# Putting the opening loads of a fused attention and MLP block on one queue, in the order of need

## The chip, the cores and the metric

The kernel runs on one core of a Trainium2 chip. The metric is the device time in microseconds (us). A number of us is the median over the fast runs of a kernel, unless the text says "profiled"; a profiled execution has a span of its own, some 1.7 us shorter than the device time of that same run. The engines are TensorE (matrix multiplications, "PE" in the profile; its weight loads are "PEld"), VectorE ("DVE"), ScalarE ("ACT"), GpSimd ("POOL") and SyncE ("SP"), which issues most transfers.

## The reference, cut to what matters

```python
x = A_x                                   # 1 x 2048 x 640, bfloat16
xn = _layernorm(x, axis=-1)               # (x - mean) / sqrt(var + eps)
return x + _A_ref(xn, A_wqkv, A_w_phi, A_wo) + _B_ref(xn, B_w1, B_w3, B_w2)
# _A_ref: qkv = xn @ wqkv; features of q and k are softmax(k @ w_phi) and softmax(-k @ w_phi) in 32 heads
#         of 20 columns; linear attention over them with v; result @ wo
# _B_ref: (silu(xn @ w1) * (xn @ w3)) @ w2
```

The 2048 tokens are 16 tiles of 128. The kernel starts from nothing, so it has an opening: the first tiles of x have to be loaded and normalised, and the weights of the features have to be folded (wk times the block diagonal of w_phi), before the main stream of projections can run.

## The kernel before: the parts that matter

The program is a list of operations (in the code cuts of this document, `...` marks what is left out, and most comments were added here). Each has a cost in us per engine that can run it, written by hand. A list scheduler plays through these costs and so decides which engine does what, and in which order. What it decided is then emitted with semaphores. A transfer is costed too, by a simple model of one shared bus. So a change to a transfer's place or cost can move instructions on every engine.

```python
POOLED = (0, 1)          # tiles whose normalisation runs on GpSimd
SEED = 0                 # the scheduler's random seed for the first 25 us
...
def bus(o, elem):        # the scheduler's cost of a transfer
    ...
    return n * 2 / elem / 16 * max(18.0, 10 + 0.0352 * elem) + 100.0
...
def ln_stats(t0, n, level):
    # DVE: bn_stats x2, bn_aggr (mean and variance); then 1/sqrt(var + eps) on GpSimd:
    ...
    add([w_op("POOL", "tensor_scalar_add", (r, v, EPS), 0.21, 0.25)], [r], [v], None, level)
    add([w_op("POOL", "tensor_tensor", (r, r, mhalf[:, 0:n], ALU.pow), 0.55 + 0.1 * (n - 1),
              0.6 + 0.1 * (n - 1))], [r], [r, mhalf[:, 0:n]], None, level)
...
def ln_apply(t, level):  # x_tok <- (x_tok - mean) * rstd, in place
    o, m, s, z = x_tok[:, t, :], mv[:, t, 0:1], mv[:, t, 4:5], mv[:, t, 6:7]
    ways = [w_op("DVE", "tensor_scalar", (o, o, m, s, ALU.subtract, ALU.mult), 0.35, 0.44)]
    if t in POOLED:
        ways = [w_op("POOL", "tensor_scalar", (o, o, m, s, ALU.subtract, ALU.mult), 1.25, 1.3)]
    ...
def block_diag(level):   # BDc: w_phi masked to a block diagonal, five products on GpSimd, read by every fold
    for c in range(DC):
        ...
        add([w_tt("POOL", o, a, b, ALU.mult, n * DH)], [o], [phi_s[:, c, :], GF[:, c, :]], None, level)
```

For the first four tiles the V projection does not wait for the normalisation. It runs on x minus its mean (`xc`, transposed to `xcT`), and the result is scaled by rstd afterwards. The K projection needs the normalised `x_tok`, transposed to `xnT`. TensorE's opening is then: transposes of xc0 and xc1, V0 and V1, transposes, V2 and V3, transposes, five folds into `Wkp`, and from there K projections and the MLP with the rest behind them.

The opening loads of before; "SP" is the default queue, and the last number in a call sets the priority:

```python
load_x(0, 1, lv)
load_x(1, 2, lv - 1)
...
load_wv(0, 2, lv - 2, "SP")
load_x(2, 3, lv - 3)
load_wv(2, 5, 2e9, "ACT")               # 480 KB at once, issued by ACT at the start
load_x(3, 4, lv - 4)
load(phi_s[:], phi_t, 2e9 - 1e3, "ACT")
for e in range(DC):
    load_wT(1, e, lv - 9 - e)           # wk, turned during the transfer: five transposes
load_w13(0, 256, lv - 16)
n = len(P.all)
load_x(4, 8, 1.9e6, "ACT")              # tiles 4-7, 640 KB
late(n, 9.0)                            # not before 9 us, by the scheduler's clock
```

The softmax here doesn't subtract the row's maximum and nothing guards it: scores larger than these inputs give would overflow.

## Time and profile before

| | before |
|---|---|
| device time, median of 3 runs (range) | 276.52 us (276.46 to 276.59) |
| span of the profiled execution | 274.9 us |
| TensorE busy | 266.7 us, 97% of the span |
| first fold starts | 15.78 us |
| first K projection starts | 17.60 us |
| from there to the end of the span | 257.3 us |

The page of before: the span, TensorE's busy time (busy us, share of the span, instructions), and the shares of the chain of waits over the whole span. That chain is followed back from the last instruction to what released it, again and again.

```profile
span 274.9 us, 5053 instructions
PE 266.7 (97%) x2078; PEld 158.9 (58%) x2097; DVE 183.1 (67%) x319; ACT 102.6 (37%) x187; POOL 65.7 (24%) x103
...
PE 91%; POOL 3%; ACT 2%; DVE 1%; issue 1%; DMA 1%
```

TensorE is the bound. In the opening, before 17.60 us, it stands idle for 3.9 us, and single holes are over 1 us long. In the 257.3 us behind that it is idle for 4.3 us in all, in short holes; the longest that its table of waits shows is 0.3 us.

The chain of waits of before, in the window from 0 to 18 us. The columns are start in us, length in us, and what it was.

```profile
by line: POOL x_tok L580 28.1%; PE PS L572 26.8%; DMA x_tok<-in_A_x_dram 12.6%; POOL mv L580 11.2%; PE PS L787 5.6%; DVE bst L580 4.9%; issue 2.6%; DVE xc L580 2.0%; PE PS L757 1.6%; DVE mv L580 0.7%
...
0.81 2.27 DMA x_tok<-in_A_x_dram
...
3.11 0.89 DVE bst L580 x2
...
5.74 2.53 POOL x_tok L580
...
8.57 0.78 POOL mv L580 x2
9.36 2.53 POOL x_tok L580
...
11.93 0.45 PE PS L787 x5
```

The opening hangs on x0's load, then on DVE's statistics, and then on GpSimd until 11.88 us. GpSimd normalises x0 (2.53 us), computes rstd of tile 1, and normalises x1 (2.53 us). No load but x0's is on this chain.

TensorE's timeline of before. The columns are start us, us, engine, line, operation, output <- inputs, shapes and count; in brackets is the idle time before it and what ended that.

```profile
6.85 2.88 PE L572 MATMUL PS<-wv,xcT 128*128 128x320 bf16 x20 [0.58 <-ACT xcT L580]
...
11.93 0.45 PE L787 MATMUL PS<-ident,x_tok 128*128 128x128 bf16 x5 [1.64 <-POOL x_tok L580]
...
15.78 1.87 PE L572 MATMUL PS<-BDc,wqkT 128*128 128x140 bf16 x30
17.60 0.85 PE L572 MATMUL PS<-Wkp,xnT 128*128 128x320 bf16 x5
```

V0 starts at 6.85, when ACT has copied xcT (6.84); wv's last piece had landed at 6.72. The longest wait that TensorE has once it works is 1.64 us, for GpSimd's x_tok. The folds start at 15.78.

GpSimd's timeline of before, first and last of its opening work, and then two lines of DVE's:

```profile
4.57 0.24 POOL L580 TENSOR_SCALAR mv<-mv 128x1 f32<-128x1 f32 x1 [2.28 <-DVE mv L580]
...
13.66 1.59 POOL L580 TENSOR_TENSOR BDc<-phi_s,GF 128x140 bf16<-128x140 bf16 x4
```

```profile
7.36 0.50 DVE L580 BATCH_NORM_STATS2 bst<-x_tok 128x6 f32<-128x320 bf16 x1 [1.16 <-DMA x_tok<-in_A_x_dram]
...
12.82 0.44 DVE L580 TENSOR_SCALAR x_tok<-x_tok,mv 128x640 bf16<-128x640 bf16 x1
```

Between these two GpSimd lines no other line has a bracket: GpSimd works without a hole from 4.57 to 15.25. DVE waits 1.16 us for the load of x2 until 7.36, and by that delays tile 1's statistics, but GpSimd is busy with x0 until 8.27 anyway. The last line shows what the same normalisation costs on DVE: 0.44 us for tile 2, against 2.53 on GpSimd.

The transfers issued by before in the first 10 us, from the profile's table of issues (output <- input, queue, kind, count, KB each, median us from issue to landing):

```profile
x_tok<-in_A_x_dram SPq DMA_DIRECT2D x4, 160.0 KB, 4.0
...
wv<-in_A_wqkv_dram ACTq DMA_DIRECT2D x1, 480.0 KB, 4.2
wv<-in_A_wqkv_dram SPq DMA_DIRECT2D x1, 320.0 KB, 5.0
```

### The profile page before, as it was taken

To read this page: it belongs to the slowest core of one execution; us is meant where nothing else is said; L and a number is where in the kernel's file an instruction comes from. 1 tells how busy PE (TensorE), PEld (TensorE's weight loads), DVE (VectorE), ACT (ScalarE), POOL (GpSimd) and SP (SyncE) were. 2 spreads that over 40 slices of the span, in tenths; PEclk is the share of its full clock that TensorE was granted. 3 is DMA by queue.
4 is the path that set the end of the run, shared out by engine and by line. 5 is a ranking of instruction groups with operands and counts; after the bars stand their busy time and mean duration, and the time that the engine had idled before them with its cause. 6 is when DMAs were issued, how large, how long until landed. Compare 5 with 4: busy or idle time off the path is not lost.

```text
span 274.9 us, 5053 instructions
## 1 busy us (share of the span) xinstructions
PE 266.7 (97%) x2078; PEld 158.9 (58%) x2097; DVE 183.1 (67%) x319; ACT 102.6 (37%) x187; POOL 65.7 (24%) x103
## 2 busy tenths in 40 slices
PE   6799999999999999999999999999999999999996
PEld 3575477656654447544444445677777774444774
DVE  4698989999957433678978978577661215666112
ACT  6379377564553451256673382010000002222000
POOL 5923556999997000000000000000000000000000
PEclk9999999999999999999999999999999999999999
DMA  7999997910000000803211111243332222000001
GB/s 216 237 317 347 195 132 129 187 67 0 2 0 2 0 0 2 284 6 27 47 26 24 38 36 24 75 99 95 97 96 75 72 72 74 0 0 0 26 24 48
DMA packets 41255, 21.98 MB, mean 80 GB/s; under 512 B 27024, under 2 KB 41232, under 8 KB 41232
## 3 DMA queue, kind: packets, MB, share of 16 engines
q1 hardware_dynamic: 39648, 20.49, 31.2%
q10 hardware_dynamic: 1584, 1.17, 1.5%
q8 instruction: 16, 0.26, 0.4%
q14 instruction: 7, 0.06, 0.1%
HBM read 12.81 MB, written 2.62 MB: 56 GB/s over the span
## 4 chain that ended last, share of the span: by engine, by line
PE 91%; POOL 3%; ACT 2%; DVE 1%; issue 1%; DMA 1%
PE PS L572 91%; POOL x_tok L580 2%; ACT EqT L580 2%; DMA x_tok<-in_A_x_dram 1%; POOL mv L580 1%; PE PS L787 0%; DVE bst L580 0%; DVE hT L580 0%; DVE den_s L580 0%; DVE xres L580 0%; ACT e_s L580 0%; DVE xc L580 0%; PE PS L757 0%; DVE t L580 0%; DVE pr_s L580 0%
## 5 line engine op out<-in xcount | busy, mean ns | idle before, releaser
L572 PE MATMUL PS<-xnT,w_s 128*128 128x512 bf16 x465 | 105.6, 379 | 1.4 <-issue 0.5
L572 PEld LDWEIGHTS PS<-xnT,w_s 128*128 128x128 bf16 x480 | 46.4, 98 | 54.5 <-DVE hT L580 0.8
L572 PE MATMUL PS<-w_s,hT 128*128 128x320 bf16 x384 | 55.0, 299 | 0.0
L580 ACT ACTIVATE th<-PS 128x512 f32<-128x512 f32 x48 | 28.7, 599 | 66.0 <-PE PS L572 66.0
L580 DVE SCALAR_TENSOR_TENSOR t<-th,PS 128x512 bf16<-128x512 f32 x48 | 32.6, 679 | 24.0 <-ACT th L580 23.9
L572 PEld LDWEIGHTS PS<-w_s,hT 128*128 128x128 bf16 x384 | 37.1, 98 | 14.9
L580 DVE TENSOR_TENSOR xres<-PS,xres 128x640 bf16<-128x640 f32 (+1 forms) x17 | 13.4, 786 | 41.2 <-PE PS L572 41.2
L580 POOL TENSOR_TENSOR ekt<-ekt,rS 128x640 bf16<-128x640 bf16 x32 | 39.6, 1275 | 1.5 <-DVE rS L580 1.5
L580 DVE SCALAR_TENSOR_TENSOR hT<-t,PS 128x512 bf16<-128x512 bf16 x48 | 32.5, 677 | 1.3 <-PE PS L572 0.3
L580 ACT ACTIVATE EqT<-PS 128x512 bf16<-128x512 f32 x40 | 21.9, 594 | 12.6 <-PE PS L572 12.6
L580 DVE TENSOR_REDUCE S<-ekt 128x64 f32<-128x1280 bf16 x16 | 22.9, 1458 | 3.4 <-ACT ekt L580 3.4
L572 PE MATMUL PS<-wo_s,oT 128*128 128x320 bf16 x160 | 24.5, 299 | 0.0
L580 DVE TENSOR_TENSOR prod<-PS,g_s 128x1280 bf16<-128x1280 f32 x16 | 23.8, 1490 | 0.5
L580 ACT ACTIVATE ekt<-PS 128x640 bf16<-128x640 f32 x32 | 20.8, 701 | 8.6 <-PE PS L572 8.4
L572 PE MATMUL PS<-Wkp,xnT 128*128 128x320 bf16 x160 | 23.9, 299 | 0.0
L572 PE MATMUL PS<-xnT,Wqp 128*128 128x512 bf16 x96 | 23.1, 380 | 0.3 <-issue 0.2
L580 ACT ACTIVATE e_s<-PS 128x64 f32<-128x64 f32 x32 | 9.1, 284 | 37.6 <-PE PS L572 37.1
L572 PEld LDWEIGHTS PS<-wo_s,oT 128*128 128x128 bf16 x160 | 15.7, 98 | 6.1
L572 PEld LDWEIGHTS PS<-Wkp,xnT 128*128 128x128 bf16 x160 | 15.5, 98 | 6.0
L572 PE MATMUL PS<-wv,xnT 128*128 128x320 bf16 x120 | 18.3, 299 | 0.0
L580 DVE BATCH_NORM_STATS2 bst<-x_tok 128x6 f32<-128x320 bf16 x32 | 14.3, 469 | 3.0 <-DMA x_tok<-in_A_x_dram 3.0
L572 PEld LDWEIGHTS PS<-xnT,Wqp 128*128 128x128 bf16 x100 | 9.3, 98 | 10.8
(68 smaller groups left out, 172.1 us busy)
## 6 DMA issues: line engine op xcount, KB each, us to landing
w_s<-in_B_w_dram SPq DMA_DIRECT2D x4, 640.0 KB, 9.2
xres<-in_A_x_dram SPq DMA_DIRECT2D x16, 160.0 KB, 2.2
out_dram<-xres SPq DMA_DIRECT2D x15, 160.0 KB, 1.8
w_s<-in_B_w_dram SPq DMA_DIRECT2D x1, 1920.0 KB, 9.2
w_s<-in_B_w_dram SPq DMA_DIRECT2D x4, 320.0 KB, 5.5
x_tok<-in_A_x_dram SPq DMA_DIRECT2D x2, 640.0 KB, 8.4
wo_s<-in_A_wo_dram SPq DMA_DIRECT2D x1, 800.0 KB, 4.9
x_tok<-in_A_x_dram SPq DMA_DIRECT2D x4, 160.0 KB, 4.0
```

Of the source, the lines that this page charges most:

```text
L572: return nc.tensor.matmul(o(u.k), l, r, start=start, stop=stop, skip_group_check=shared)
L580: return getattr(e, name)(*[at(a, u) for a in args], **{k: at(v, u) for k, v in kw.items()})
```

## The change

The intent is that data which is needed first should land first. The big 480 KB piece of wv no longer runs beside x0 and x1, on ACT's queue. It is cut in two and put behind them on SP's queue. phi and tiles 4 to 7 are issued later. The scheduler's bus model and its seed are changed as well.

```diff
-SEED = 0
+SEED = 1
...
-        return n * 2 / elem / 16 * max(18.0, 10 + 0.0352 * elem) + 100.0
+        return n * 2 / elem / 16 * max(18.0, 12 + 0.0375 * elem) + 100.0
...
     load_wv(0, 2, lv - 2, "SP")
     load_x(2, 3, lv - 3)
-    load_wv(2, 5, 2e9, "ACT")
-    load_x(3, 4, lv - 4)
-    load(phi_s[:], phi_t, 2e9 - 1e3, "ACT")
+    load_wv(2, 3, lv - 4, "SP")
+    load_wv(3, 5, lv - 5, "SP")
+    load_x(3, 4, lv - 6)
+    n = len(P.all)
+    load(phi_s[:], phi_t, 2e9, "ACT")
+    late(n, 4.0)
     for e in range(DC):
         load_wT(1, e, lv - 9 - e)
     load_w13(0, 256, lv - 16)
     n = len(P.all)
     load_x(4, 8, 1.9e6, "ACT")
-    late(n, 9.0)
+    late(n, 10.3)
```

Because the schedule is built anew, instructions move too. A comparison of the two built programs shows it. On GpSimd, tile 2's rstd comes before x1's normalisation, and tile 3's comes before the first BDc block. On TensorE, tile 1's transpose stands directly before V2, and behind the folds its matmuls come in the same order as before. DVE has one copy less in the opening and two instructions less in all, which ACT takes over, and a different order. No arithmetic of the block is added or removed; TensorE gets five more of the warm-up matmuls on zeros that it runs before V0 (22 instead of 17).

## The prediction

> **What bounds the kernel now.** TensorE: the page gives it 266.7 of 274.9 us (97%), the chain of waits is 91% matmuls of line 572. From 17.60 us (first K projection) the timeline shows TensorE almost without a hole, at clock 1.00. So only the opening can give anything: whatever moves the folds (15.78 us) and K (17.60 us) moves the end nearly one for one.
>
> **What bounds the opening.** The chain of waits: x0's load 0.81 to 3.08, DVE statistics to 4.5, then GpSimd: 0.25 + 0.76 (rstd of tile 0), 2.53 (normalise x0), about 1.0 (rstd 1), 2.53 (normalise x1) to 11.88; then TensorE: transposes, V2 and V3 (2.72), transposes, folds. The timeline shows GpSimd without a hole from 4.57 to 15.25, when the last BDc block (needed by the first fold) is done. TensorE's longest wait, 1.6 us, is for GpSimd's x_tok. The loads bind less: V0 starts at 6.85, when wv's SP piece lands (1.73 + 5.0), and DVE waits 1.2 us for x2 until 7.36, which holds tile 1's statistics until 7.95; but GpSimd is busy until 8.27.
>
> **What the change does.** wv's 480 KB on ACT's queue moves behind x0, x1, wv[0:2], x2 on SP's. Per the Trainium skill (DMA: Bandwidth & Descriptors, "Issuing engines are not separate DMA queues") both run on the same 16 engines and interleave. The trace agrees: x1 needed about 3 us, x0 2.27. 1305 KB landed between 3.08 and 7.8 us, some 280 KB per us. Estimates from that and 0.45 us per issue: x1 3.6 (was 4.3), wv[0:2] 4.8 (6.7), x2 5.4 (7.3), wv[3:5] 7.1, x3 7.7. V0 starts near 6.3, tile 1's statistics end near 6.5. x0 gains almost nothing: it took 2.27, the same 160 KB as xres 2.2.
>
> The price: weight transposes issue 0.6 us later (last lands near 14.5, needed near 16); tiles 4-7 land near 16 (needed 18.2). Both have slack.
>
> Rebuilding the schedule reorders instructions. On GpSimd, tile 2's rstd (0.24 + 0.75, partly overlapped) now stands before x1's normalisation, tile 3's before the first BDc. Same work, same start: x0 done 8.27, rstd 1 and 2 until 10.05, x1 done near 12.6 (was 11.88), BDc done near 15.5. TensorE now has tile 1's transpose directly before V2 and V3: 12.65 + 0.28 + 2.72 + 0.28 = 15.95 for the folds, against 15.78. What the loads win (0.5 us at V0, 1.5 us at tile 1's statistics) turns into a longer wait for GpSimd. Behind the folds TensorE's order is the same.
>
> **Prediction.** -0.1 (x0) + 0.15 (folds) and jitter: 276.5 us; 275.7 to 277.3 in 8 of 10 cases. Faster by over 2%: 1%; within: 98%; slower: 1%.
>
> **Signs.** Right: x1, wv[0:2], x2 land 0.7 to 2 us sooner; V0 starts before 6.6; GpSimd gapless from about 4.5 to 15.5; x1's normalisation starts near 10.1; TensorE waits over 1 us for x_tok before V2; K starts at 17.4 to 18.1. Wrong: GpSimd has a hole or its normalisation gets shorter than 2.53; K before 17.2.
>
> **What would make it wrong.** Faster: x0 lands sooner, moving the whole GpSimd chain, or rstd 2 overlaps more. Slower: from 9.7 to 12.6 TensorE does only short transposes; the skill (TensorE: Matmul & The Clock Gate, Part 1) has the clock halved after an idle window of about 3.4 us. The 1.64 us hole here did not slow V2; a longer one could, costing up to 2.7 us. Or late weight transposes delay the folds.

## The result and the profile after

| | before | after |
|---|---|---|
| device time, median of 4 runs | 276.55 us | 276.93 us |
| range | 276.46 to 276.84 | 276.74 to 276.99 |
| span of the profiled execution | 274.9 us | 275.3 us |
| first fold starts | 15.78 us | 15.95 us |
| first K projection starts | 17.60 us | 17.66 us |
| from there to the end of the span | 257.3 us | 257.6 us |

The ratio is 1.0011, with a 95% interval from 0.9993 to 1.0028: the same within 2%, and not resolved from 1. A ratio here is the mean time of one kernel's fast runs over that of the other's of the same rounds, so it is not quite the ratio of the medians that are quoted.

The page of after:

```profile
span 275.3 us, 5067 instructions
PE 267.4 (97%) x2083; PEld 159.1 (58%) x2102; DVE 180.7 (66%) x317; ACT 103.7 (38%) x189; POOL 65.7 (24%) x103
...
PE 78%; DVE 10%; POOL 5%; issue 3%; ACT 2%; DMA 1%; POOLq 0%; DVEq 0%
```

TensorE does the same work but for the five warm-up matmuls. But DVE's share of the chain of waits went from 1% to 10%, so something in the main stream now touches DVE. That comes back below.

The transfers that after issued in its first 10 us:

```profile
x_tok<-in_A_x_dram SPq DMA_DIRECT2D x4, 160.0 KB, 3.0
wv<-in_A_wqkv_dram SPq DMA_DIRECT2D x2, 320.0 KB, 4.3
wv<-in_A_wqkv_dram SPq DMA_DIRECT2D x1, 160.0 KB, 3.6
```

The change did to the loads what it meant to: a tile of x now takes 3.0 us (median) instead of 4.0. The Trainium skill says in "DMA: Bandwidth & Descriptors", section "Issuing engines are not separate DMA queues", that transfers started by different engines run on the same 16 engines and interleave. This trace agrees: with the 480 KB of wv no longer issued beside it, x1 needed about 2.3 us instead of about 3.

The chain of waits of after, 0 to 18 us:

```profile
0.81 2.24 DMA x_tok<-in_A_x_dram
...
5.54 2.66 POOL x_tok L580
...
8.50 0.79 POOL mv L580 x2
...
9.36 0.64 POOL mv L580
...
10.01 2.53 POOL x_tok L580
...
12.68 0.44 PE PS L787 x5
```

It is the same chain. The step at 9.36 is new: rstd of tile 2 stands ahead of x1's normalisation, which starts at 10.01 instead of 9.36. Such times on GpSimd are rough, but the wait that they cause on TensorE is not. TensorE's timeline of after:

```profile
6.14 0.98 PE L572 MATMUL PS<-wv,xcT 128*128 128x320 bf16 x6
8.22 2.06 PE L572 MATMUL PS<-wv,xcT 128*128 128x320 bf16 x14 [1.10 <-DMA wv<-in_A_wqkv_dram]
...
11.11 0.45 PE L787 MATMUL PS<-ident,x_tok 128*128 128x128 bf16 x5 [0.27 <-DVE x_tok L580]
...
12.68 0.44 PE L787 MATMUL PS<-ident,x_tok 128*128 128x128 bf16 x5 [0.81 <-POOL x_tok L580]
...
15.95 1.87 PE L572 MATMUL PS<-BDc,wqkT 128*128 128x140 bf16 x30
17.66 0.72 PE L572 MATMUL PS<-Wkp,xnT 128*128 128x320 bf16 x4
```

V0 starts 0.71 us sooner, then stalls 1.10 us for the last piece of wv, which landed at about 8.1. Part of the earlier start is luck. The warm-up matmuls come at half pace at first (one of 128 columns every 0.11 us, later every 0.056), and how long that lasts differs from profile to profile: the last slow one started at 3.8 us in before, at 4.4 in after, but at 6.0 in phi_later and 6.8 in order_only, which come below. In after_x4_early, with the same loads before V0, V0 started at 6.93. Whatever is left of the gain is waited off at 12.68, for GpSimd. The folds start 0.17 us later than before, and K 0.06 us.

The other quarter of a microsecond lies far from the opening. TensorE's and DVE's timelines of before, around 63 us, with DVE's last two hT (a block of the MLP's hidden layer):

```profile
63.72 1.52 PE L572 MATMUL PS<-Wkp,xnT 128*128 128x320 bf16 x10
```

```profile
58.49 0.62 DVE L580 SCALAR_TENSOR_TENSOR hT<-t,PS 128x512 bf16<-128x512 bf16 x1
...
63.28 0.62 DVE L580 SCALAR_TENSOR_TENSOR hT<-t,PS 128x512 bf16<-128x512 bf16 x1
```

The same of after, and the only wait of TensorE's weight loads that its table of waits shows between 33 and 68 us (total us, times, longest):

```profile
63.78 1.78 PE L572 MATMUL PS<-Wkp,xnT 128*128 128x320 bf16 x10
```

```profile
63.48 0.62 DVE L580 SCALAR_TENSOR_TENSOR hT<-t,PS 128x512 bf16<-128x512 bf16 x1
```

```profile
PEld PS L572 <- DVE hT L580: 0.3, 1, 0.3
```

In both programs the first two matmuls of this K projection each wait for DVE, because they write to banks that DVE has to have read first: the second waits for an hT. But it is not the same hT. The two programs, built anew, show it. Both write this projection to the same two banks, but the MLP blocks ahead of it got their banks in another turn. So in before the bank was last read by the hT of 58.49, which had ended at 59.11, and in after by the next hT, the one of 63.48. In before the second matmul's weights are loaded at 63.72, while the hT of 63.28 still runs, and ten matmuls take 1.52 us. In after TensorE arrives only 0.06 us later, but its second weight load stands idle until that hT ends, and starts at 64.15. The ten matmuls take 1.78 us, a hole of about 0.26 us. It comes from the turn of the banks, not from a slower DVE. This and the 0.06 us of K make up the 0.3 to 0.4 us between the two spans. The hole also explains the 10% of DVE: from it the chain of waits is followed back along DVE and what feeds it, to about 28.7 us. So a tenth of the chain stands for a loss of 0.26 us.

### The profile page after: what moved, and what is told of

The parts are those of the page before. It is cut to its first block, busy times and chain, and to the rows that moved or that the text cites. A ratio compares the mean times of both kernels' runs of the same rounds, so it can differ in the third digit from the quotient of the medians.

```text
span 275.3 us, 5067 instructions
## 1 busy us (share of the span) xinstructions
PE 267.4 (97%) x2083; PEld 159.1 (58%) x2102; DVE 180.7 (66%) x317; ACT 103.7 (38%) x189; POOL 65.7 (24%) x103
## 4 chain that ended last, share of the span: by engine, by line
PE 78%; DVE 10%; POOL 5%; issue 3%; ACT 2%; DMA 1%; POOLq 0%; DVEq 0%
PE PS L572 78%; DVE S L580 4%; POOL mv L580 2%; POOL x_tok L580 2%; ACT EqT L580 2%; DVE hT L580 1%; DVE rS L580 1%; DVE bst L580 1%; DMA x_tok<-in_A_x_dram 1%; DVE t L580 1%; DVE x_tok L580 0%; ACT th L580 0%; ACT x_tok L580 0%; DVE mv L580 0%; POOL epsc L580 0%
## 5 line engine op out<-in xcount | busy, mean ns | idle before, releaser
L580 ACT ACTIVATE th<-PS 128x512 f32<-128x512 f32 x48 | 28.7, 597 | 65.7 <-PE PS L572 65.6
L572 PEld LDWEIGHTS PS<-Wkp,xnT 128*128 128x128 bf16 x160 | 15.4, 98 | 6.2 <-DVE hT L580 0.3
```

Source lines behind the costliest of these rows:

```text
L572: return nc.tensor.matmul(o(u.k), l, r, start=start, stop=stop, skip_group_check=shared)
L580: return getattr(e, name)(*[at(a, u) for a in args], **{k: at(v, u) for k, v in kw.items()})
```

## The experiments

In all experiments that move loads or instructions, the schedule of one kernel was kept as it was computed and only the named items were moved in it, so that the other engines keep their order. Every kernel gave a correct result. Before ran beside each of them, at 276.55 to 276.62 us. "K" is the start of the first K projection in the profiled execution, and "rest" is that span less K.

| kernel | median us (runs) | range | ratio to before, 95% | K | rest |
|---|---|---|---|---|---|
| before | 276.55 (4) | 276.46 to 276.84 | | 17.60 | 257.3 |
| after | 276.93 (4) | 276.74 to 276.99 | 1.0011, 0.9993 to 1.0028 | 17.66 | 257.6 |
| loads_only | 278.06 (6) | 277.43 to 280.89 | 1.0068, 1.0038 to 1.0099 | 19.56 | 257.3 |
| order_only | 276.99 (5) | 276.78 to 277.09 | 1.0012, 0.9999 to 1.0025 | 17.77 | 257.5 |
| phi_later | 276.91 (5) | 276.86 to 276.97 | 1.0011, 0.9999 to 1.0023 | 17.68 | 257.5 |
| norm_dve_after | 275.66 (5) | 275.50 to 275.83 | 0.9966, 0.9954 to 0.9978 | 16.56 | 257.3 |
| loads_only_again | 277.72 (4) | 276.45 to 277.91 | 1.0029, 1.0011 to 1.0046 | 18.64 | 257.4 |
| loads_only_filled | 277.49 (6) | 276.74 to 278.89 | 1.0032, 1.0013 to 1.0051 | 18.46 | 257.3 |
| norm_dve_before | 275.46 (6) | 275.22 to 276.31 | 0.9961, 0.9949 to 0.9974 | 16.37 | 257.3 |
| true_cost_after | 276.86 (5) | 276.70 to 277.15 | 1.0009, 0.9997 to 1.0021 | 18.05 | 257.3 |
| loads_only_x4_late | 277.23 (6) | 276.72 to 278.29 | 1.0030, 1.0013 to 1.0047 | 17.62 | 258.7 |
| after_x4_early | 276.85 (5) | 276.73 to 276.94 | 1.0011, 0.9998 to 1.0024 | 17.44 | 257.7 |
| norm_dve_wv_first | 276.15 (5) | 275.80 to 276.30 | 0.9981, 0.9967 to 0.9994 | 17.00 | 257.4 |

Each K and rest comes from one profiled execution. K differs by 0.2 us between profiles of one order (17.44 in after_x4_early, 17.68 in phi_later), so differences of 0.1 us are not resolved. The column "rest" already says much: it is 257.3 or 257.4 in every kernel but two kinds. It is 257.5 to 257.7 wherever after's order of instructions is kept, and 258.7 in one kernel that starves DVE.

The theory was: GpSimd's normalisation of x0 and x1 bounds the opening, so loads that land sooner are waited off there. The rivals were: the loads do bind, and the change gives with one hand what it takes with the other (x sooner, the end of wv and the weight transposes later); or it is the new order of instructions that costs what the loads win.

### loads_only: the new loads, with before's order on every compute engine

```diff
--- before
+    # the schedule stands; only the opening loads are moved
+    wv_2, wv_34 = piece(2, 3), piece(3, 5)        # SP, behind x2's load, instead of the 480 KB on ACT
+    ...                                           # each matmul waits for the piece that it reads
+    move(phi_load, acts[1])
+    move(x4_load, acts[6])
```

> The changed kernel's loads under the earlier kernel's instruction order on every compute engine. Theory A (GpSimd's gapless chain sets the opening, loads do not bind; the added 0.3 us came from the reordering): x1, wv[0:2] and x2 land as early as in the changed kernel, but GpSimd is gapless from about 4.5 to 15.2 us, K starts at 17.5 to 17.7, no hole before the K tile at 63.7 us, time 276.3 to 276.7 (ratio to the kernel before 0.999 to 1.001). Theory B (the loads bind, and what they gained was lost because wv[3:5] and x3 landed about a us later than estimated): the late wv[3:5] stalls V0 here too, so K starts 0.3 us or more later than 17.60.

It was slower than both kernels: 278.06 us, ratio 1.0068. Theory B had expected a late K, but through a stall of V0 for wv, and of that this profile shows at most 0.2 us. The profiled run has two lines that explain its own time. TensorE's timeline, V2 and V3:

```profile
12.90 4.55 PE L572 MATMUL PS<-wv,xcT 128*128 128x320 bf16 x20
```

And busy time by stretches of 1 us (the stretch and its length; then TensorE, weight loads, DVE, ACT, GpSimd; then the granted clock of TensorE, DMA share and GB/s):

```profile
10.00:11.00 1.00, 0.25 (x5) 0.07 (x2) 0.90 (x3) 0.53 (x1) 1.00 (x1) 1.00 0.82 139
11.00:12.00 1.00, 0.00 (x0) 0.00 (x0) 0.00 (x0) 0.00 (x0) 1.00 (x1) 1.00 0.76 83
...
13.00:14.00 1.00, 1.00 (x9) 0.60 (x6) 0.76 (x3) 0.70 (x1) 1.00 (x3) 0.70 0.97 120
14.00:15.00 1.00, 1.00 (x5) 0.60 (x4) 0.48 (x1) 0.00 (x0) 1.00 (x3) 0.50 1.04 154
...
16.00:17.00 1.00, 1.00 (x6) 0.56 (x5) 0.00 (x0) 0.10 (x1) 0.00 (x0) 0.59 1.15 303
```

TensorE stood idle for 2.08 us until 12.33, again waiting for GpSimd's x_tok, and then the granted clock fell to a half. V2 and V3 took 4.55 us, where before needed 2.88. If the clock is taken to be either full or half, the shares 0.70, 0.50, 0.50 (in the line from 15 to 16 us too) and 0.59 add up to 3.4 us at half clock. But the clock was low in only two of the six runs (278.65 and 280.89 us), and the other four were still 277.43 to 278.11. Something else costs about 1 us.

### loads_only_again and loads_only_filled: is it the clock?

The first is the same kernel under another name. The second fills the hole with 28 dummy matmuls.

```diff
--- loads_only
+    # dummy matmuls into the hole between the transposes of tile 0 and tile 1
+    for n in range(28):
+        o = _Op({"PE": (lambda: nc.tensor.matmul(bank(7, 128), zero[:, 0:128], zero[:, 0:128], start=True,
+                                                 stop=True), 0.056, 0.2)})
+        ...
```

> The same kernel as loads_only, to see whether its slowness (278.06 against an expected 276.5) comes back and whether its cause is one thing. Its first profile had the granted clock at 0.5 from about 13 to 16.3 us, and V2 and V3 took 4.55 instead of 2.88 us, after a TensorE hole of 2.08 us; but four of its six runs reported a mean clock of 1.000 and were still 0.9 to 1.6 us slow. Clock theory: this profile shows again matmuls of V2 and V3, or others of the opening, at double time, even if the mean clock reads 1.000. Rival (a wait): all matmuls at full rate and a new hole of 0.9 us or more.

> loads_only with 28 dummy matmuls of 128 columns (1.6 us at full rate) put into TensorE's hole between the transposes of tile 0 and tile 1. They compute nothing that is used. Clock theory: TensorE no longer idles, V2 and V3 run at 2.7 to 2.9 us, the spread of the runs shrinks below 0.5 us, time 276.3 to 276.9. That would also finish the test of theory A: the new loads under the old order give K at 17.5 to 18.0 and no gain. Rival (a wait, or theory B): the time stays at 277.4 or more.

They were 277.72 and 277.49 us, and in the profiled run of each the clock stayed at 1.00. So filling the hole is no cure, and the clock is not the main cause. The fill was not quite free either: x1 was ready at about 12.0 us there, and the dummies held TensorE until 12.44. The profiled run of loads_only_again shows another cause, in the middle of the first fold:

```profile
17.18 1.50 PE L572 MATMUL PS<-BDc,wqkT 128*128 128x140 bf16 x25 [0.83 <-DMA wqkT<-in_A_wqkv_dram]
```

The last transpose of wk landed only at 17.1 us, 7.3 us after its issue. The same transpose needed 5.1 us in before (8.9 to 14.0), 6.1 in after (9.8 to 15.9), 8.1 in loads_only and 6.8 in loads_only_filled (fold wait 0.31 us). In loads_only itself no fold waited for it, because the low clock had already put the folds back to 17.85. The last transpose is first read by the sixth matmul of the first fold, as the five before the hole show. In after that matmul's weights were loaded at 16.14, so the transpose, landing at 15.85, had about 0.3 us to spare.

### loads_only_x4_late and after_x4_early: what makes the transposes late?

In loads_only the 640 KB load of tiles 4 to 7 is issued from ACT while the transposes are under way. A collision was the next theory.

```diff
--- loads_only
-    move(x4_load, acts[6])
+    move(x4_load, acts[7])          # issued at 12.84 us, behind the last transpose
--- after (the second kernel)
+    P.ops.remove(x4_load)           # issued at 9.08 us instead of 10.60
+    P.ops.insert(P.ops.index(acts[5]) + 1, x4_load)
```

> loads_only with the one load of token tiles 4-7 (640 KB, ACT's queue) issued two ACT instructions later, near 12 to 13 us instead of 9.7 to 10.5. In loads_only and its repeats the first fold waited for the last weight transpose, which landed at 16.8 to 17.5 us instead of 14.0[...]. Collision theory: with the load out of the way the last weight transpose lands by 15.4, no TensorE wait for it, K starts at 17.5 to 17.8, runs spread less than 0.5 us, time 276.3 to 276.8; that is the remaining part of theory A (new loads, old order, no gain). If the transposes are late for another reason (the single queue itself): they still land after 16 us and the time stays at 277.3 or more.

> The changed kernel with only tiles 4-7 issued two ACT instructions sooner, near 9.0 us instead of 10.6, so without the third part of the change. Its weight transposes run from 4.2 to about 15.9 us. Collision theory: the load now meets more of the transposes; the last one lands at 16.3 or later, the first fold waits for it, K after 18.0, 277.2 or more with a wide spread. If the late issue does nothing: the time stays at 276.7 to 277.0 and K at 17.6 to 17.7.

With the load out of the way the last transpose took 3.2 us instead of 8.1, the fold waited for nothing, and K started at 17.62, as in before. So the collision makes the transposes late in loads_only, as far as one profiled execution of each shows it; the runs of loads_only_again spread from 276.45 to 277.91, so the delay is not the same each time. Yet the kernel was no faster than before: its runs lie from 276.72 to 278.29. In the profiled run, one of the slowest (278.04), tiles 4 to 7 now came too late for DVE, in its timeline:

```profile
20.95 0.89 DVE L580 BATCH_NORM_STATS2 bst<-x_tok 128x6 f32<-128x320 bf16 x2 [2.66 <-DMA x_tok<-in_A_x_dram]
```

From there the delay reached TensorE, which waited 0.60 us for DVE at 28.15; the rest grew by 1.4 us to 258.7. The reverse in after did no harm at all: the last transpose took 5.0 us and K started at 17.44. So the collision is not a rule as it was worded.

The 13 profiles together say more. What goes with the time of the last transpose is how long before or behind it the 640 KB load is issued. Issued 0.5 to 0.8 us before it, the transpose took 5.0 to 5.1 us (before, norm_dve_before, after_x4_early); within 0.2 us of it, 5.8 and 6.1 (order_only, true_cost_after); about 0.4 to 0.5 us behind it, 6.8 to 8.1 (the three loads_only kernels); 0.8 to 0.9 us behind, 5.9 to 6.1 (after, phi_later); and 1.3 us or more behind, 3.2 to 3.4 (norm_dve_after, norm_dve_wv_first, loads_only_x4_late), although the transpose was still under way. No run changed the spacing in small steps, so this is a pattern and not a tested cause, and why it should matter stays open.

### order_only: after's order, with the old loads

```diff
--- after
+    # the schedule stands; only the opening loads are moved back
+    for o, a, b in ((wv_2, 2, 3), (wv_34, 3, 5)):
+        o.eng = "ACT"
+        o.emit = lambda a=a, b=b: nc.scalar.dma_start(wv[:, a:b, :], wqkv_t[:, a:b, 2 * D:3 * D])
+    move(phi_load, acts[0])
+    move(wv_34, acts[0])
+    move(wv_2, acts[0])
+    move(x4_load, acts[5])
```

> The changed kernel's instruction order with wv[2:5] and phi back on ACT's queue at the start (wv[2:5] still in two pieces). Theory A: the time is that of the changed kernel although the loads are the earlier ones: x1's normalisation on GpSimd again starts near 10.0, K at 17.6 to 17.8, the hole of about 0.25 us before the K tile at 63.8 us remains, 276.7 to 277.0. Theory B: V0 runs 0.5 us sooner to its end than in the changed kernel (9.6 instead of 10.1) and K follows, at 17.3 or earlier, 276.2 to 276.5.

It took 276.99 us, within 0.06 us of after. V0 started late again (7.11; here the long slow warm-up delays it too) and ran without a stall, and TensorE again waited 0.81 us for GpSimd's x_tok; K started at 17.77. The hole at 63.89 us was there (1.75 us for ten matmuls), with the same wait for DVE's hT. In loads_only, which has the new loads and the old order and banks, that wait was absent. So the hole belongs to the rebuilt schedule, not to the loads, and the loads alone, within after's order, are worth at most 0.1 us at K, which single profiles do not resolve.

### phi_later: take the stall for wv away

```diff
--- after
+    # the schedule stands; only phi is issued three ACT instructions later
+    P.ops.remove(phi_load)
+    P.ops.insert(P.ops.index(acts[4]) + 1, phi_load)
```

> The changed kernel with only phi's load issued about 3 us later on ACT, everything else in place. If phi's many small packets (its queue's packets against bytes in the trace) delayed wv[3:5] and x3: wv[3:5] lands near 7.2 instead of 8.2, x3 near 7.8 instead of 8.8, TensorE's 1.1 us wait for wv disappears, V1 ends about 1 us sooner. If it is the single queue that is slow: nothing moves. Theory A: even when that 1.1 us hole goes, K still starts at 17.6 to 17.8, because GpSimd's x1 is done at 12.5 as before; time 276.7 to 277.0. Theory B: K starts 0.5 to 1 us sooner, 276.0 to 276.4.

The wv piece landed at about 7.8 instead of 8.1, not at the 7.2 that was expected. But TensorE's stall for wv fell from 1.10 to 0.19 us, because V0 also started later (6.74), behind a longer slow warm-up. K was at 17.68 and the time 276.91 us: unchanged. With GpSimd on the path, the stall of V0 does not bind.

### norm_dve_after and norm_dve_before: take GpSimd off the path

```diff
--- after, and the same edit in before
-POOLED = (0, 1)
+POOLED = ()
```

This lets DVE normalise x0 and x1 too. The schedule is built anew.

> The changed kernel with the normalisation of x0 and x1 on DVE (about 0.45 us each) instead of GpSimd (2.5 us each); the schedule is rebuilt. Theory A: GpSimd loses about 5 us of work and gets holes before 14 us; K starts 0.7 to 1.5 us sooner (16.1 to 16.9), time 275.4 to 276.2. Theory B: V0 and V1 keep ending near 10.1 because of wv[3:5], and K moves by less than 0.3 us, 276.5 to 277.

> The kernel before (wv on ACT's queue) with the normalisation of x0 and x1 on DVE, schedule rebuilt: the fourth corner of loads against GpSimd. Theory A with loads of no worth: as fast as norm_dve_after within 0.4 us (275.3 to 276.1), K at 16.3 to 16.9. If the loads begin to bind once GpSimd is out of the way (the change's intent is right but masked): slower than norm_dve_after by 0.5 us or more, 276.2 or more.

| median us | before's loads | after's loads |
|---|---|---|
| x0 and x1 normalised on GpSimd | 276.55 | 276.93 |
| x0 and x1 normalised on DVE | 275.46 | 275.66 |

Moving two operations off GpSimd is worth 1.1 us with the old loads and 1.3 us with the new ones. Moving the loads brings no gain in either row. The rebuild moves other instructions too, so the 1.1 and 1.3 us need not be GpSimd's alone; but true_cost_after, below, is rebuilt as well, with GpSimd's work kept, and gains nothing. The chain of waits of norm_dve_before, 0 to 18 us, shows the loads as the next bound:

```profile
by line: PE PS L572 50.1%; DMA wv<-in_A_wqkv_dram 27.6%; PE PS L787 7.0%; SPq L642 4.5%; PE PS L757 4.1%; issue 1.8%; PE PS L1027 0.9%
...
1.73 4.97 DMA wv<-in_A_wqkv_dram
```

GpSimd is gone from it, and wv's load, landing at 6.70, stands there. In norm_dve_after the same place is held by wv's last piece, issued at 3.18 and landing at 7.93. So once the loads do bind, the new order of loads is not the better one: it delivers x sooner and wv later, and wv is what TensorE waits for there. norm_dve_before has the lowest median, 0.39% under before, and is faster than after as well; against norm_dve_after (0.34%) it is not resolved.

### norm_dve_wv_first: wv ahead of x2

```diff
--- norm_dve_after
+    # the schedule stands; only x2's load goes behind the last piece of wv
+    P.ops.remove(x2_load)
+    P.ops.insert(P.ops.index(wv_34) + 1, x2_load)
```

> norm_dve_after with x2's load moved behind the last piece of wv on SP's queue, every other instruction in place. In both kernels with the normalisation on DVE the chain of waits goes through wv's load (landed 6.70 with the two queues, 7.93 on the one queue), no longer through GpSimd. If the loads bind now: wv lands near 7.2 to 7.5, V0 shows no wait or a short one, V1 ends near 9.7 instead of 10.1, K starts 0.2 to 0.5 us sooner than 16.56, time 275.2 to 275.5. If something else binds (DVE's statistics of x2, which now lands later, or the weight transposes): K within 0.1 us of 16.56, 275.5 to 275.9.

V1 ended sooner (9.38 instead of 10.1), but the time was 276.15 us, slower than norm_dve_after, and K was at 17.00. The wait had moved, as DVE's timeline shows:

```profile
8.06 0.89 DVE L580 BATCH_NORM_STATS2 bst<-x_tok 128x6 f32<-128x320 bf16 x2 [1.84 <-DMA x_tok<-in_A_x_dram]
```

x2 now landed at 8.04, and V2 waited for its statistics. In this opening both wv and x2 are wanted at the same time, so an order of loads only chooses which one is late.

### true_cost_after: tell the scheduler what GpSimd takes

```diff
--- after
-            ways = [w_op("POOL", "tensor_scalar", (o, o, m, s, ALU.subtract, ALU.mult), 1.25, 1.3)]
+            ways = [w_op("POOL", "tensor_scalar", (o, o, m, s, ALU.subtract, ALU.mult), 2.5, 2.55)]
```

> The changed kernel with one number of the scheduler's cost table changed: GpSimd's normalisation 2.5 us instead of 1.25. GpSimd keeps the same work. The rebuilt order puts V2 and V3 ahead of tile 1's transpose, so TensorE no longer waits for x1 before V2. Theory A: what is left is GpSimd's last BDc block near 15.3 to 15.6 us, which the first fold needs; K at 16.9 to 17.4, time 276.1 to 276.6. If instead only the wait for x1 had counted: K at 16.5 or earlier, 275.8 or less.

The scheduler then let TensorE run V2 (10.00) without waiting for x1, as was hoped. But K came at 18.05, later than in after, and the time was 276.86 us. The folds had to wait for GpSimd's last products, in its timeline:

```profile
14.48 2.05 POOL L580 TENSOR_TENSOR BDc<-phi_s,GF 128x140 bf16<-128x140 bf16 x5
```

They ended at 16.53, and the folds took 2.44 us instead of 1.87. The expected gain was missed, but GpSimd again set the start of K. That the time is no worse than after's fits the rest of 257.3 us: in this schedule the hole at 63.8 us is gone.

## Why the prediction was right or wrong

The time was right: 276.5 us predicted with a range from 275.7 to 277.3, and 276.93 measured. Point by point:

- **GpSimd bounds the opening, and the old loads do not: shown.** The chain of waits of after is the same as that of before, and the rebuild with the normalisation off GpSimd moved K by 1.1 to 1.2 us, while the loads within after's order moved it by 0.1. Within before's order the new loads gained nothing either, but there they could do harm: K came up to 2.0 us later in the loads_only kernels, through the weight transposes and, in two runs, the clock.
- **The arithmetic of the opening: right.** x1's normalisation was expected at 10.05 to 10.1 and started at 10.01. The folds were expected at 15.95 and started at 15.95. K was expected between 17.4 and 18.1 and started at 17.66. GpSimd had no hole from 4.53 to 15.4. Tile 1's statistics ended at 6.45, expected near 6.5.
- **x0 lands hardly sooner: right.** 2.24 us against 2.27. The 0.1 us that the sum credited for it was 0.03.
- **The step that failed: "Behind the folds TensorE's order is the same", with only jitter allowed for it.** TensorE's order is the same there, but the turn of its banks is not, and so neither is the DVE instruction that it waits for: the hT that ended at 64.1 instead of one that had ended at 59.1. That cost about 0.26 us in one K projection at 63.8 us, a term that the sum does not have. order_only keeps it with the old loads, and loads_only does not have it with the new ones. Of the 0.4 us by which the prediction was low, this is most.
- **Landing times mis-sized.** wv[3:5] landed at about 8.1 (estimated 7.1), x3 at about 8.8 (7.7), wv[0:2] at 5.4 (4.8), and the last weight transpose at 15.9 (14.5). V0 did start before 6.6, as expected, but with luck (6.74 in phi_later, 6.93 in after_x4_early), and the prediction did not see that it would then stall 1.10 us. None of this reached K in after. The transposes, though, had about 0.3 us of slack and not the 1.5 that was claimed; in loads_only they did delay the folds, which the prediction had named among the dangers.
- **"TensorE waits over 1 us for x_tok before V2": 0.81 us** for GpSimd's x_tok, and 0.27 for DVE's x_tok ahead of it.
- **The clock.** The prediction named a longer hole as a risk. It did not happen in after. It did happen in loads_only, in two of six runs, after a hole of 2.08 us.

What stays open is why the weight transposes take between 3 and 8 us beside much the same other loads, depending on when the 640 KB load is issued.

## What to carry to other kernels

Before the loads of an opening are put in a better order, look in the chain of waits for what stands between the first load and the first real matmul: here it was 5 us of normalisation on GpSimd, which DVE did in about 0.5 us a tile, and moving that was worth more than any order of loads. In a kernel whose order a scheduler computes, a change of loads is also a change of order on every engine, and of the banks that TensorE waits for; hold one fixed and move the other before either is believed. A load order that is good for one consumer is paid for by another, so list what each piece releases, and how much slack the last piece really has, before it is moved back.

## What the Trainium skill lacked or had wrong

- "GPSIMD Engine Reference", section 4.1, "Engine selection", calls GpSimd about twice as slow for two-input elementwise operations and says "1-input is roughly line-rate". Here a one-input operation, (x - m) * r with two values per partition on 128x640 bfloat16, took 2.52 to 2.71 us on GpSimd and 0.44 us on DVE, a factor of about 6.
- "TensorE: Matmul & The Clock Gate", Part 1, has a free-running window of about 3.4 us: the first one is at half rate, and the clock is halved again after an idle one. The length agreed (3.4 us at half clock in loads_only). But the clock fell at about 13.4 us there (worked out from the share 0.70), and in the 3.4 us before that TensorE was busy for about 1.3 us by the table of stretches, so if that was the window, it need not be wholly idle. At the start, the recorded clock was 1.00 all the time although matmuls came at half pace: in loads_only_again five 128-column transposes took 0.74 us at 5.82, and 0.44 us later on. The page does warn that these records can't be fully trusted.
- "DMA: Bandwidth & Descriptors", section "Rules for kernel authors", says that a transpose "next to ordinary DMAs needs nothing". That is said of correctness, and every result here was correct. It gives no cost in time. The last transpose of a 640x128 block took 3.2 us with the 640 KB load of tiles 4 to 7 out of its way (loads_only_x4_late). Beside that load it took 5.0 to 6.1 us in before, after and after_x4_early, and 6.8 to 8.1 in the three loads_only kernels; with the load issued 1.3 us behind it, 3.4 us (norm_dve_after).
